# Attention and two MLPs on one core: TensorE's next instruction goes to the half of the rows that a count calls free first

## The chip, the cores and the metric

The kernel runs on one core of one Trainium2 chip. The metric is the device time of one execution in microseconds (us); the kernel before takes 653.88 us, the median of three runs (653.44 to 654.54).

## The reference, cut to what matters

```python
def _attn_ref(q, k, v):                      # (2, 8, 1152, 64) each
    q_pool = q.reshape(B, H, S // 2, 2, D).mean(axis=3)
    scores = np.matmul(q_pool, k.transpose(0, 1, 3, 2)) / np.sqrt(D)
    scores = scores - np.max(scores, axis=-1, keepdims=True)
    attn = np.exp(scores)
    attn = attn / (np.sum(attn, axis=-1, keepdims=True) + 1e-09)
    return np.matmul(attn, v)

x = attn_out.transpose(0, 2, 1, 3).reshape(1152, 512)
x = (s * np.maximum(x @ w_in, 0) ** 2 + b) @ w_out          # d_ff 2048
x = ((x @ w_a) * (x @ w_b)) @ w_out2                        # d_ff 1536
```

The change touches the attention alone: 16 heads of 576 pooled queries by 1152 keys, 64 deep, in float32.

## The kernel before, in words

The heads are worked off in eight pairs. A pair has nine blocks of 128 queries (four of each head, and one that holds the last 64 queries of both). For one block *g* the steps, with the names of the table SCHED, are:

- **S** (`s_mm`): scores against 1024 of the keys, two float32 matmuls of 512 columns. The contraction is 64 deep, so one matmul uses the lower half of TensorE's rows (partitions 0 to 63, the even chunks of keys) and the other the upper half (64 to 127, the odd chunks); the two run at the same time. **SX** (`s_mmx`): the last 128 keys, one matmul in one half only; both halves hold these keys, and before, odd blocks use the upper half and even blocks the lower.
- **M, MX, C** (VectorE): maximum over the scores; **X, XX** (ScalarE): exp with its sum; **A, R** (VectorE): the sum's reciprocal; **N** (GpSimd): the row is scaled.
- **T** (`p_tr`): the scaled block is transposed chunk by chunk, 64 rows of it at a time: eight transposes in the lower half into one PSUM tile, eight in the upper half into another. **H** copies the lower half's tile to `pt` (ScalarE, line 357), **D** the upper half's (VectorE, line 353). There is one such tile for each half, so the next group of transposes in a half waits for that copy.
- **U.0 to U.3** (`turns`): the transposes of the ninth chunk of several blocks, with those of the next pair's keys or queries riding along; **UH** and **UD** copy them out.
- **P0, P1** (`pv_mm`): attention times values, over all 128 rows.

SCHED is one period of a software pipeline, written out by hand; the marks behind a name say how many pairs it lags. `steps()` expands it, and each step is recorded in that order, so every engine's queue is in the order of the program. An engine waits for another by semaphores; TensorE adds to its semaphore behind the last transpose of each half (for H and for D) and behind the second half of an S.

In every step before, the halves simply take turns: `turn` issues lower, upper, lower, upper, and S lower, upper. The place in the period on which most turns is, in the table, `SX.8 T.4 S.7 SX.7 ... U.1 ... P0.0`: on TensorE an SX, a group of 16 transposes, an S, another SX, the 14 transposes of U.1, and then P0. It comes once in each pair's period. Behind the attention stand the two MLPs, in full rows, which the change doesn't touch.

Of the kernel before, what the change touches and what calls it, by code (L numbers as in the profile page):

```python
# [9 lines left out]
F32 = mybir.dt.float32  # L10
# [26 lines left out]
def kernel(  # L37
# [14 lines left out]
    nc = tc.nc  # L52
    B, H, S, D = q.shape
# [24 lines left out]
    ident = const.tile([128, 128], F32, name="ident")  # L78
# [176 lines left out]
    s01 = ctx.enter_context(ExitStack())  # L255
    ps_s01 = s01.enter_context(tc.tile_pool(name="ps_s01", bufs=2, space=PSUM))
# [3 lines left out]
    NE = 7  # L260
    e_all = nc.alloc_sbuf_tensor("e", [128, 3, S], F32, side="right")
    qp_all = nc.alloc_sbuf_tensor("qpl", [128, 9, 2, D], F32, side="right")
    e_at = [e_all.ap()[:, i] for i in range(3)]
# [13 lines left out]
    def bank(key, reads):  # L277
        held[key] = [free.pop(0), reads]
        return banks[held[key][0]].tile([128, 512], F32, tag="b", name="b")
# [6 lines left out]
    QN, QM, KN, VN, X, Q, QT = {}, {}, {}, {}, {}, {}, {}  # L286
    HALF = [slice(0, 64), slice(64, 128)]

    def bh(n):
        return n // HP, 2 * (n % HP)  # L290

    def load_q(n, part=0, queue=nc.sync):
        if n >= NP:
            return
        b, h = bh(n)
        if part < 2:
            QN[n] = nat.tile([128, 2, 4, 2, D], F32, tag="qn", name="qn")
        o = slice(max(part - 1, 0), 2 if part != 1 else 1)
        queue.dma_start(
            out=QN[n][:, o], in_=q[b, h + o.start:h + o.stop, 0:1024, :].rearrange("h (p j r) d -> p h j r d", p=128, j=4)  # L300
        )
        if part != 1:
            QM[n] = nat.tile([128, 2, D], F32, tag="qm", name="qm")
            for i in range(2):
                queue.dma_start(out=QM[n][HALF[i]], in_=q[b, h + i, 1024:S, :].rearrange("(p r) d -> p r d", r=2))

    def load_k(n, part=0):
        if n >= NP:
            return
        b, h = bh(n)  # L310
        if part < 2:
            KN[n] = k_p.tile([128, 2, NC + 1, D], F32, tag="kn", name="kn")
        o = slice(max(part - 1, 0), 2 if part != 1 else 1)
        src = k[b, h + o.start:h + o.stop].rearrange("h (p c) d -> p h c d", p=128)
        nc.sync.dma_start(out=KN[n][:, o, 0:NC], in_=src)
        nc.sync.dma_start(out=KN[n][:, o, NC], in_=src[:, :, NC - 1])

    def load_v(n):
        if n >= NP:
            return  # L320
        b, h = bh(n)
        VN[n] = v_p.tile([128, 2, NC, D], F32, tag="vn", name="vn")
        nc.sync.dma_start(out=VN[n], in_=v[b, h:h + 2].rearrange("h (p c) d -> p h c d", p=128))
# [11 lines left out]
    def q_step(n, hd):  # L335
        q_pool(n, hd)
        if hd == 1:
            q_pool(n, 2)
            load_q(n + 1)

    def turn(ps, z, src):
        for o, t in zip(HALF, ps):
            nc.tensor.transpose(t[:, z * 64:z * 64 + 64], src(o), ident[o, o])  # L343

    def by_half(t, n, k):
        return t.rearrange("p (m k e) -> p k m e", m=n, k=2)[:, k]
# [15 lines left out]
    SPS, XPS, SM, PS = {}, {}, {}, {}  # L362

    def s_parts(g):
        n, i = divmod(g, 9)
        hd, j = ORDER[i]

        def mm(ps, w, r, c):
            o = HALF[r]
            if hd < 2:  # L370
                nc.tensor.matmul(ps[:, 0:w], Q[n, hd][o, j * 128:(j + 1) * 128], X[n, hd][o, c], start=True, stop=True)  # L371
            else:
                for a in range(2):
                    nc.tensor.matmul(ps[HALF[a], 0:w], Q[n, 2][o, a], X[n, a][o, c], start=True, stop=True, skip_group_check=True)  # L374

        return mm

    def s_mm(g):
        SPS[g] = ps = ps_s01.tile([128, 2, 512], F32, tag="s01", name="s01")
        for r in range(2):  # L380
            s_parts(g)(ps[:, r], 512, r, slice(0, 512))

    def s_mmx(g):
        XPS[g] = ps = bank(("x", g), 2)
        s_parts(g)(ps, 128, g % 2, slice(512, 640))

    def small(g):
        if g not in SM:
# [36 lines left out]
    def t_tiles(key):  # L425
        PS[key] = [p.tile([128, 512], F32, tag="t", name="t") for p in ps_t]
        return PS[key]

    def p_turn(ps, g, z, pos):
        turn(ps, z, lambda o: e_at[g % NE][o, pos * 128:(pos + 1) * 128])  # L430

    def p_tr(g):
        ps = t_tiles(g)
        for pos in range(8):
            p_turn(ps, g, pos, pos)

    def p_col(j):
        return j * 128 if j < 2 else j * 128 + NX
# [13 lines left out]
    def turns(n, u):  # L452
        at = TURN[u] if n >= 0 else ()
        if not at and n + 1 >= NP:
            return
        ps = t_tiles((n, u))
        for z, i in enumerate(at):
            p_turn(ps, 9 * n + i, z, 8)
        if n + 1 < NP:
            z, hd = len(at), u // 2  # L460
            if u % 2:
                src = qp_all.ap()
                for j in range(4):
                    turn(ps, z + j, lambda o: src[o, 4 * hd + j].rearrange("p a d -> p (a d)"))
                if hd:
                    turn(ps, z + 4, lambda o: src[o, 8].rearrange("p a d -> p (a d)"))
                    Q[n + 1, 2] = q_p.tile([128, 2, 64], F32, tag="qt", name="qt")
                Q[n + 1, hd] = q_p.tile([128, 512], F32, tag=f"q{hd}", name="q")
            else:

                for m in range(5):
                    turn(ps, z + m, lambda o: KN[n + 1][o, hd, 2 * m:2 * m + 2].rearrange("p a d -> p (a d)"))
                X[n + 1, hd] = x_p.tile([128, 640], F32, tag=f"x{hd}", name="x")
                if hd:
                    load_k(n + 3)

    def turns_last(n, u, k):
        if n < 0:
# [18 lines left out]
    def turns_out(k):  # L497
        def run(n, u):
            turns_last(n, u, k)
            turns_ride(n, u, k)  # L500

        return run
# [4 lines left out]
    def pv_mm(n, hd, pos):  # L507
        if pos == 0:
            PV[n, hd] = bank(("pv", n, hd), 4 if (n, hd) == (NP - 1, 1) else 1)
        ps = PV[n, hd]  # L510
        for a in range(2):
            nc.tensor.matmul(  # L512
                ps[HALF[a], 0:HC], VN[n][:, hd, CHUNK[pos]], pt[:, hd, pos, a * HC:(a + 1) * HC],
                start=(pos == 0), stop=(pos == NC - 1), skip_group_check=True,
            )
        if hd and pos == NC - 1:
            load_v(n + 2)
# [34 lines left out]
    def block(f, *z):  # L552
        return lambda n, i: f(9 * n + i, *z)

    def conv_until(n, i):
# [3 lines left out]

    STEPS = dict(  # L560
        S=block(s_mm), SX=block(s_mmx), M=block(s_max), MX=block(s_maxx), C=block(s_comb), X=block(s_exp), XX=block(s_expx),
        A=block(s_add), R=block(s_rec), N=block(s_norm), T=block(p_tr), H=block(p_evac, 0), D=block(p_evac, 1),
        U=turns, UH=turns_out(0), UD=turns_out(1), QP=q_step, PVc=pv_copy, PVd=pv_move, XS=x_split, CV=conv_until,
    )
    for name in ("MM", "Fa", "Fd", "Fp"):
        STEPS[name] = lambda n, i: next(up_down)
    for hd in range(2):
        STEPS[f"P{hd}"] = lambda n, pos, hd=hd: pv_mm(n, hd, pos)

    def steps():  # L570

        lag = [(t.rstrip("',"), t.count("'") - t.count(",")) for t in SCHED]
        lags = [s for _, s in lag]
        first = dict(QP=1, CV=NP - 1, MM=NP - 1, Fa=NP - 1, Fd=NP - 1, Fp=NP - 1, U=-1, UH=-1, UD=-1)
        for p in range(min(lags) - 1, NP + max(lags)):
            for t, s in lag:
                if first.get(t.split(".")[0], 0) <= p - s < NP:
                    yield t, p - s

    def step(t, n):  # L580
        name, i = t.split(".")
        STEPS[name](n, int(i))
# [12 lines left out]
    with tc.manual_schedule():  # L595
# [13 lines left out]
        for t in early:  # L609
            step(t, -1)  # L610
# [4 lines left out]
        unit_load()  # L615
        load_v(1)
        order = [(t, n) for t, n in steps() if n >= 0 or t not in early]
        end = 1 + max(i for i, (t, n) in enumerate(order) if t.split(".")[0] in ("S", "SX"))
        for t, n in order[:end]:
            step(t, n)  # L620
# [150 lines left out]
        for t, n in order[end:]:  # L771
            step(t, n)
# [19 lines left out]
        def pair(i):  # L792
            return ps2[i].tile([128, 2, 512], F32, tag="pp", name="pp")
# [22 lines left out]
        U = {}  # L816
# [43 lines left out]
        at = [at_t[:, i] for i in range(2)]  # L860
# [26 lines left out]
        def o_room(i):  # L887
            return ab_at(i)[:, 256 + NX:256 + NX + DM]
# [17 lines left out]
        a, c, b, d = (pair(i) for i in range(4))  # L906
# [37 lines left out]
        for n in range(1, NU):  # L944
# [3 lines left out]
            a = pair(2)  # L948
# [46 lines left out]
        ps = [t[:, i] for t in (pair(i) for i in (2, 3, 1, 0)) for i in range(2)]  # L995
# [21 lines left out]
        o = o_room(8)  # L1017
# [33 lines left out]
```

## Time and profile before

| what | number |
|---|---|
| median of the runs | 653.88 us |
| the profiled execution | 653.54 us, of which the span of its instructions is 651.8 us |
| TensorE matmul busy | 637.7 us, 98% of the span |
| VectorE, ScalarE, GpSimd busy | 464.9, 332.5 and 276.5 us |
| TensorE's granted clock | full in all 40 slices |
| attention | from the start to some 238 us |
| one pair's period in the steady part | 27.74 to 27.80 us |

The page cuts the span into 40 slices and gives each engine's busy share. The timeline lists instructions in order of time: start, length, engine, line, operation, how many were merged into the row, and in brackets how long the engine had been idle and what ended it. Matmuls overlap, since a record runs from the start to the last result; where two halves work, rows of both lie over each other. A float32 matmul of 512 or 128 columns makes two passes and has two records, a transpose has one. Line numbers are those of the kernel before.

### The profile page before, as it was taken

The page shows a single profiled execution, that of the slowest core. Times are in us where ns is not written, and L with a number is a line of the kernel's source. Part 1 is how long each engine was busy: PE and PEld are TensorE (multiplying, and loading weights), DVE is VectorE, ACT ScalarE, POOL GpSimd, SP SyncE. Part 2 cuts the span into 40 slices and gives each one's busy share as a digit, 9 for nine tenths or more (in the row PEclk, how much of TensorE's full clock was granted, in tenths as well). Part 3 has the DMA queues.
Part 4 walks back from the last instruction along what each step waited for, and adds up shares of the span by engine and source line. Part 5 has one row for each costly group of instructions (what it writes and reads, how often), then busy time and mean ns, then how long its engine had stood idle before and what let it go on. Part 6 is the DMA issues. An engine that isn't in the chain of part 4 may idle for free.

```text
span 651.8 us, 13010 instructions
## 1 busy us (share of the span) xinstructions
PE 637.7 (98%) x5182; PEld 537.6 (82%) x5182; DVE 464.9 (71%) x892; ACT 332.5 (51%) x697; POOL 276.5 (42%) x228
## 2 busy tenths in 40 slices
PE   7899999999999999999999999999999999999997
PEld 5556666565665679999999999999999999988885
DVE  5888888888888845735456465889887887796431
ACT  4777778778787724535224224244434343533321
POOL 3545466564654566855355354200542453230000
PEclk9999999999999999999999999999999999999999
DMA  8313140431302044232232132500323131323004
GB/s 264 105 41 98 37 133 19 115 91 45 93 8 60 10 140 129 75 121 65 67 127 65 66 129 66 180 15 0 131 69 126 65 130 66 130 71 123 1 0 146
DMA packets 30509, 55.75 MB, mean 86 GB/s; under 512 B 4336, under 2 KB 7280, under 8 KB 30448
## 3 DMA queue, kind: packets, MB, share of 16 engines
q1 hardware_dynamic: 29920, 54.19, 25.8%
q8 instruction: 41, 0.67, 0.4%
q10 hardware_dynamic: 528, 0.72, 0.3%
q14 instruction: 20, 0.16, 0.1%
HBM read 50.33 MB, written 2.36 MB: 81 GB/s over the span
## 4 chain that ended last, share of the span: by engine, by line
PE 92%; DVE 4%; ACT 2%; POOL 1%; issue 1%; POOLq 0%; DVEq 0%; ACTq 0%
PE ps L592 31%; PE pp L592 18%; PE pp L885 11%; PE b L512 11%; PE t L343 9%; PE s L371 8%; PE b L371 2%; PE s L374 1%; DVE sm L393 1%; ACT e L406 1%; PE t L606 1%; DVE e L827 1%; PE b L374 0%; POOL e L423 0%; DVE wl L160 0%
## 5 line engine op out<-in xcount | busy, mean ns | idle before, releaser
L423 POOL TENSOR_SCALAR e<-e,sm 128x1152 f32<-128x1152 f32 x72 | 87.8, 1225 | 89.2 <-DVE sm L401 57.4
L393 DVE TENSOR_REDUCE sm<-s 128x1 f32<-128x1024 f32 x72 | 87.9, 1220 | 10.8 <-PE s L371 6.6
L406 ACT ACTIVATE e<-s,sm 128x1024 f32<-128x1024 f32 x72 | 80.5, 1118 | 13.6 <-DVE sm L401 12.7
L343 PEld LDWEIGHTS t<-ident,e 64*128 64x128 f32 x1296 | 59.1, 138 | 29.3 <-issue 9.7
L512 PE MATMUL b<-pt,vn 128*64 128x288 f32 x576 | 81.8, 416 | 0.1
L371 PE MATMUL s<-x,q 64*128 64x512 f32 x256 | 72.8, 624 | 3.1 <-ACT e L406 2.5
L353 DVE COPY pt<-t 128x512 f32<-128x512 f32 (+1 forms) x112 | 59.7, 539 | 22.0 <-PE t L343 21.8
L900 POOL TENSOR_TENSOR ab<-ab,at 128x576 f32<-128x576 f32 x24 | 35.0, 1480 | 91.1 <-ACT ab L895 87.2
L343 PE MATMUL t<-ident,e 64*128 64x64 f32 x1296 | 69.4, 228 | 4.3 <-POOL e L423 2.4
L512 PEld LDWEIGHTS b<-pt,vn 128*64 128x64 f32 x576 | 36.6, 136 | 31.9 <-ACT e L410 6.1
L357 ACT COPY pt<-t 128x512 f32<-128x512 f32 (+1 forms) x112 | 51.5, 469 | 19.3 <-PE t L343 18.6
L699 POOL TENSOR_SCALAR r<-r,sb_s,sb_b 128x384 f32<-128x384 f32 (+1 forms) x46 | 38.9, 856 | 51.8 <-DVE r L696 51.8
L693 ACT ACTIVATE qpl<-ps 128x384 f32<-128x384 f32 (+1 forms) x46 | 21.7, 503 | 69.4 <-PE ps L592 64.6
L696 DVE SCALAR_TENSOR_TENSOR r<-ps,qpl 128x384 f32<-128x384 f32 (+1 forms) x46 | 25.1, 571 | 38.4 <-ACT qpl L693 38.4
L136 ACT ACTIVATE f<-raw 128x1024 f32<-128x1024 f32 x34 | 38.6, 1135 | 17.7 <-issue 11.1
L592 PE MATMUL ps<-xa_h,wh 128*128 128x384 f32 (+1 forms) x200 | 45.3, 330 | 0.0
L592 PE MATMUL ps<-xa_h,wl 128*128 128x384 f32 (+1 forms) x200 | 45.0, 329 | 0.0
L592 PE MATMUL ps<-xa_l,wh 128*128 128x384 f32 (+1 forms) x200 | 45.0, 328 | 0.0
L140 DVE SCALAR_TENSOR_TENSOR f<-raw,f 128x1024 int32<-128x1024 int32 x34 | 43.0, 1263 | 1.1
L592 PE MATMUL ps<-gh,wh 128*128 128x384 f32 x192 | 43.7, 336 | 0.0
L592 PE MATMUL ps<-gh,wl 128*128 128x384 f32 x192 | 43.7, 336 | 0.0
L592 PE MATMUL ps<-gl,wh 128*128 128x384 f32 x192 | 43.7, 336 | 0.0
(115 smaller groups left out, 1490.3 us busy)
## 6 DMA issues: line engine op xcount, KB each, us to landing
raw<-in_moe_w_out_dram SPq DMA_DIRECT2D x14, 1024.0 KB, 4.9
raw<-in_moe_w_in_dram SPq DMA_DIRECT2D x8, 1024.0 KB, 5.4
raw<-in_moe_w_a_dram SPq DMA_DIRECT2D x6, 1024.0 KB, 5.1
raw<-in_moe_w_b_dram SPq DMA_DIRECT2D x6, 1024.0 KB, 5.1
vn<-in_v_dram SPq DMA_DIRECT2D x8, 576.0 KB, 5.9
kn<-in_k_dram SPq DMA_DIRECT2D x7, 576.0 KB, 3.9
qn<-in_q_dram SPq DMA_DIRECT2D x7, 512.0 KB, 3.8
xs<-tmp SPq DMA_DIRECT2D x30, 72.0 KB, 4.9
```

Of the source, the lines that this page charges most:

```text
L140: nc.vector.scalar_tensor_tensor(out=f, in0=lo, scalar=29, in1=f, op0=ALU.logical_shift_right, op1=ALU.bitwise_or)
L343: nc.tensor.transpose(t[:, z * 64:z * 64 + 64], src(o), ident[o, o])
L353: nc.vector.tensor_copy(out=out, in_=in_)
L357: nc.scalar.copy(out=out, in_=in_)
L371: nc.tensor.matmul(ps[:, 0:w], Q[n, hd][o, j * 128:(j + 1) * 128], X[n, hd][o, c], start=True, stop=True)
L393: nc.vector.reduce_max(small(g)[:, 0:1], SPS[g], axis=AX.XY)
L406: nc.scalar.activation(out=out, in_=SPS.pop(g), func=AF.Exp, bias=m[:, 2:3], accum_out=m[:, 4:5])
L423: nc.gpsimd.tensor_scalar(out=e, in0=e, scalar1=m[:, 6:7], scalar2=1.0, op0=ALU.mult, op1=ALU.mult)
L512: nc.tensor.matmul(ps[HALF[a], 0:HC], VN[n][:, hd, CHUNK[pos]], pt[:, hd, pos, a * HC:(a + 1) * HC], start=(pos == 0), stop=(pos == NC - 1 ...
L592: nc.tensor.matmul(ps, a, c[:, o:o + n], start=(first and z == 0), stop=(last and z == 2), skip_group_check=more)
L699: nc.gpsimd.tensor_scalar(out=r2, in0=r2, scalar1=sb_s, scalar2=sb_b, op0=ALU.mult, op1=ALU.add)
L885: nc.tensor.matmul(ps, a[x], w2_at[kf][c], start=(kf == 0 and y == 0), stop=(kf == KF2 - 1 and y == 2))
```

## The change

While the program is written, three numbers are kept: for each half, when it would be free, and when the last instruction was issued. A transpose counts 63, a half of S 960, an SX 218. `lanes` takes a list of instructions for each half and always issues next the one whose half is free first. The SX goes to the half that is free first, instead of by the block's number. `together` levels the count, before P and around the ninth block. The order of the steps is kept, with one exception: where a group T is followed by its S with nothing between that this S needs, `look_ahead` puts the two into one list, so that one half may start its S while the other still has transposes to issue.

```diff
+    clock = [0, 0, 0]
+
+    def lanes(*todo):
+        todo = [list(x) for x in todo]
+        while todo[0] or todo[1]:
+            r = min((r for r in range(2) if todo[r]), key=lambda r: (clock[r], len(todo[r]) < len(todo[1 - r])))
+            cost, run = todo[r].pop(0)
+            clock[2] = max(clock[r], clock[2])
+            clock[r] = clock[2] + cost
+            run()
+
+    def together():
+        clock[:] = [max(clock)] * 3
+
     def turn(ps, z, src):
-        for o, t in zip(HALF, ps):
-            nc.tensor.transpose(t[:, z * 64:z * 64 + 64], src(o), ident[o, o])
+        def one(o, t):
+            return 63, lambda: nc.tensor.transpose(t[:, z * 64:z * 64 + 64], src(o), ident[o, o])
+
+        return [one(o, t) for o, t in zip(HALF, ps)]
...
+    def s_halves(g):
+        SPS[g] = ps = ps_s01.tile([128, 2, 512], F32, tag="s01", name="s01")
+        mm = s_parts(g)
+        return [[(960, lambda r=r: mm(ps[:, r], 512, r, slice(0, 512)))] for r in range(2)]
+
     def s_mm(g):
-        SPS[g] = ps = ps_s01.tile([128, 2, 512], F32, tag="s01", name="s01")
-        for r in range(2):
-            s_parts(g)(ps[:, r], 512, r, slice(0, 512))
+        if g in SPS:
+            return
+        if g % 9 == 4:
+            together()
+        lanes(*s_halves(g))
 
     def s_mmx(g):
         XPS[g] = ps = bank(("x", g), 2)
-        s_parts(g)(ps, 128, g % 2, slice(512, 640))
+        if g % 9 == 4:
+            together()
+        r = int(clock[1] < clock[0])
+        todo = [[], []]
+        todo[r] = [(218, lambda: s_parts(g)(ps, 128, r, slice(512, 640)))]
+        lanes(*todo)
+        if g % 9 == 4:
+            together()
...
     def p_tr(g):
         ps = t_tiles(g)
-        for pos in range(8):
-            p_turn(ps, g, pos, pos)
+        todo = turns_both([p_turn(ps, g, pos, pos) for pos in range(8)])
+        if g in AHEAD:
+            for x, y in zip(todo, s_halves(AHEAD[g])):
+                x += y
+        lanes(*todo)
...
@@ def pv_mm(n, hd, pos):
+        together()
...
+    def look_ahead(order):
+
+        for i, (t, n) in enumerate(order):
+            name, z = t.split(".")
+            if name != "T":
+                continue
+            wait = set()
+            for u, m in order[i + 1:]:
+                next_name, y = u.split(".")
+                g = 9 * m + int(y)
+                if next_name in ("SX", "T", "U", "P0", "P1", "MM"):
+                    break
+                if next_name == "S":
+                    if y != "4" and not wait & {("X", g - 2), ("U", g // 9 - 1)}:
+                        AHEAD[9 * n + int(z)] = g
+                    break
+                wait.add(("X", g) if next_name == "X" else ("U", m) if next_name in ("UH", "UD") else None)
```

`turns` (U) gathers its transposes in the same way and hands them to `lanes`. The queues of the other engines and of the DMAs keep their order; only names of buffers differ there.

On TensorE, the first steady place `SX.8 T.4 S.7 SX.7 U.1` stood so before (b is an SX, the transposes t read the scaled block e_96, s_927 is the S; lower and upper half take turns in each row of more than one; in brackets the semaphores that the first instruction of a row waits for):

```order
L371 MATMUL b<-x,q 128x128 [waits Activation_49]
L343 MATMUL t<-ident,e_96 128x64 [waits PE_49,Pool_49]
L343 MATMUL t<-ident,e_96 128x64 [waits DVE_49]
L343 MATMUL t<-ident,e_96 128x64 x14
L371 MATMUL s_927<-x,q 128x512 [waits Activation_49]
L371 MATMUL s_927<-x,q 128x512
L371 MATMUL b<-x,q 128x128 [waits Activation_49]
```

And it stands so in the changed kernel, where the same S is called s_911; the first SX is in the lower half here:

```order
L392 MATMUL b<-x,q 128x128 [waits Activation_49]
L359 MATMUL t<-ident,e_96 128x64 [waits DVE_49,Pool_49]
L359 MATMUL t<-ident,e_96 128x64 x3
L359 MATMUL t<-ident,e_96 128x64 [waits PE_49]
L359 MATMUL t<-ident,e_96 128x64 x8
L392 MATMUL s_911<-x,q 128x512 [waits Activation_49]
L359 MATMUL t<-ident,e_96 128x64 x3
L392 MATMUL s_911<-x,q 128x512
L392 MATMUL b<-x,q 128x128 [waits Activation_49]
```

The first four transposes are now all in the upper half, the S of the upper half has moved ahead of three transposes, and these three are the last of the lower half.

A place with an S and one SX ahead of U (here U.0's transposes: e and e_93 are blocks of this pair, kn the next pair's keys) stood so before:

```order
L371 MATMUL s_785<-x,q 128x512 x2
L371 MATMUL b<-x,q 128x128
L343 MATMUL t<-ident,e 128x64 x2
L343 MATMUL t<-ident,e_93 128x64 x2
L343 MATMUL t<-ident,kn 128x64 x10
L512 MATMUL b<-pt,vn 64x288 x4
```

In the changed kernel, where this S is s_766, it stands so:

```order
L392 MATMUL s_766<-x,q 128x512 x2
L392 MATMUL b<-x,q 128x128
L359 MATMUL t<-ident,e 128x64
L359 MATMUL t<-ident,e_93 128x64
L359 MATMUL t<-ident,kn 128x64 x2
L359 MATMUL t<-ident,e 128x64
L359 MATMUL t<-ident,kn 128x64
L359 MATMUL t<-ident,e_93 128x64
L359 MATMUL t<-ident,kn 128x64 x7
L512 MATMUL b<-pt,vn 64x288 x4
```

The half without the SX has been moved ahead by four transposes; its last four no longer stand at the end, where those of the other half are now alone.

## Rows read from the trace of the kernel before

**Rows 1.** The page: busy time of the engines, and granted clock in 40 slices.

```profile
PE 637.7 (98%) x5182; PEld 537.6 (82%) x5182; DVE 464.9 (71%) x892; ACT 332.5 (51%) x697; POOL 276.5 (42%) x228
PEclk9999999999999999999999999999999999999999
```

**Rows 2.** Busy time in two periods: PE, PEld, DVE, ACT, POOL, PEclk, DMA share, GB/s.

```profile
57.29:85.09 27.80, 27.78 (x334) 17.15 (x336) 23.89 (x65) 21.36 (x58) 15.96 (x15) 1.00 0.28 80
85.09:112.83 27.74, 27.72 (x335) 17.16 (x336) 23.80 (x65) 21.45 (x58) 15.82 (x15) 1.00 0.28 78
```

**Rows 3.** The timeline of TensorE from SX.8 to P0.0, first SX in the upper half.

```profile
110.42 0.37 PE L371 MATMUL b<-x,q 64*128 64x128 f32 x1
110.52 0.28 PE L343 MATMUL t<-ident,e 64*128 64x64 f32 x1
...
111.08 0.65 PE L371 MATMUL s<-x,q 64*128 64x512 f32 x1
111.12 0.29 PE L343 MATMUL t<-ident,e 64*128 64x64 f32 x2
111.24 1.07 PE L371 MATMUL s<-x,q 64*128 64x512 f32 x3
...
112.19 0.40 PE L343 MATMUL t<-ident,e 64*128 64x64 f32 x6
...
112.76 0.46 PE L512 MATMUL b<-pt,vn 128*64 128x288 f32 x2
```

**Rows 4.** The same place a period earlier, first SX in the lower half.

```profile
82.62 0.37 PE L371 MATMUL b<-x,q 64*128 64x128 f32 x1
82.73 0.27 PE L343 MATMUL t<-ident,e 64*128 64x64 f32 x1
...
83.32 0.69 PE L371 MATMUL s<-x,q 64*128 64x512 f32 x1
83.38 0.22 PE L343 MATMUL t<-ident,e 64*128 64x64 f32 x1
...
84.35 0.22 PE L343 MATMUL t<-ident,e 64*128 64x64 f32 x1
...
85.02 0.46 PE L512 MATMUL b<-pt,vn 128*64 128x288 f32 x2
```

**Rows 5.** ScalarE's timeline at both places: the copy H.4, then XX.8 and X.8.

```profile
111.39 0.59 ACT L357 COPY pt<-t 128x512 f32<-128x512 f32 x1 [0.22 <-PE t L343]
...
83.64 0.58 ACT L357 COPY pt<-t 128x512 f32<-128x512 f32 x1 [0.27 <-PE t L343]
84.12 0.37 ACT L410 ACTIVATE e<-b,sm 128x128 f32<-128x128 f32 x1
```

**Rows 6.** VectorE's timeline at both places: C.8, then the copy D.4.

```profile
111.28 0.15 DVE L401 TENSOR_REDUCE sm<-sm 128x1 f32<-128x2 f32 x1
111.44 0.69 DVE L353 COPY pt<-t 128x512 f32<-128x512 f32 x1
...
83.47 0.15 DVE L401 TENSOR_REDUCE sm<-sm 128x1 f32<-128x2 f32 x1
83.67 0.69 DVE L353 COPY pt<-t 128x512 f32<-128x512 f32 x1
```

**Rows 7.** GpSimd's timeline: N.4, the scaling of the block that T.4 reads.

```profile
109.24 1.22 POOL L423 TENSOR_SCALAR e<-e,sm 128x1152 f32<-128x1152 f32 x1 [3.82 <-DVE sm L401]
```

**Rows 8.** TensorE's timeline in the first pair: T.4, and P0.0 after it.

```profile
27.12 0.71 PE L343 MATMUL t<-ident,e 64*128 64x64 f32 x16 [1.64 <-POOL e L423]
...
29.32 0.47 PE L512 MATMUL b<-pt,vn 128*64 128x288 f32 x2
```

**Rows 9.** TensorE's timeline, T, S, SX and U.0 up to P1: SX in the upper half.

```profile
74.03 0.71 PE L343 MATMUL t<-ident,e 64*128 64x64 f32 x16
...
76.24 0.46 PE L512 MATMUL b<-pt,vn 128*64 128x288 f32 x2
```

**Rows 10.** The same place a period later, SX in the lower half.

```profile
101.83 0.71 PE L343 MATMUL t<-ident,e 64*128 64x64 f32 x16
...
104.03 0.46 PE L512 MATMUL b<-pt,vn 128*64 128x288 f32 x2
```

More of the change, by code (lines that the diff above doesn't have):

```diff
@@ L339, in q_step, with turns_both @@
             load_q(n + 1)
-    def turn(ps, z, src):
-        for o, t in zip(HALF, ps):
-            nc.tensor.transpose(t[:, z * 64:z * 64 + 64], src(o), ident[o, o])
+    clock = [0, 0, 0]
[9 more added lines that the diff above has]
+        clock[:] = [max(clock)] * 3
+    def turn(ps, z, src):
+        def one(o, t):
+            return 63, lambda: nc.tensor.transpose(t[:, z * 64:z * 64 + 64], src(o), ident[o, o])
+        return [one(o, t) for o, t in zip(HALF, ps)]
+    def turns_both(items):
+        return [[x[r] for x in items] for r in range(2)]
     def by_half(t, n, k):
@@ L429, in p_turn @@
     def p_turn(ps, g, z, pos):
-        turn(ps, z, lambda o: e_at[g % NE][o, pos * 128:(pos + 1) * 128])
+        return turn(ps, z, lambda o: e_at[g % NE][o, pos * 128:(pos + 1) * 128])
+    AHEAD = {}
     def p_tr(g):
         ps = t_tiles(g)
-        for pos in range(8):
-            p_turn(ps, g, pos, pos)
+        todo = turns_both([p_turn(ps, g, pos, pos) for pos in range(8)])
[3 more added lines that the diff above has]
+        lanes(*todo)
     def p_col(j):
@@ L456, in turns @@
         ps = t_tiles((n, u))
-        for z, i in enumerate(at):
-            p_turn(ps, 9 * n + i, z, 8)
+        items = [p_turn(ps, 9 * n + i, z, 8) for z, i in enumerate(at)]
         if n + 1 < NP:
@@ L462, in turns @@
                 src = qp_all.ap()
-                for j in range(4):
-                    turn(ps, z + j, lambda o: src[o, 4 * hd + j].rearrange("p a d -> p (a d)"))
+                for j in [4 * hd + j for j in range(4)] + [8] * hd:
+                    items.append(turn(ps, len(items), lambda o, j=j: src[o, j].rearrange("p a d -> p (a d)")))
                 if hd:
-                    turn(ps, z + 4, lambda o: src[o, 8].rearrange("p a d -> p (a d)"))
                     Q[n + 1, 2] = q_p.tile([128, 2, 64], F32, tag="qt", name="qt")
@@ L471, in turns @@
                 for m in range(5):
-                    turn(ps, z + m, lambda o: KN[n + 1][o, hd, 2 * m:2 * m + 2].rearrange("p a d -> p (a d)"))
+                    items.append(turn(ps, z + m, lambda o, m=m: KN[n + 1][o, hd, 2 * m:2 * m + 2].rearrange("p a d -> p (a d)")))
                 X[n + 1, hd] = x_p.tile([128, 640], F32, tag=f"x{hd}", name="x")
-                if hd:
-                    load_k(n + 3)
+        lanes(*turns_both(items))
+        if u == 2:
+            load_k(n + 3)
     def turns_last(n, u, k):
@@ L617 @@
         order = [(t, n) for t, n in steps() if n >= 0 or t not in early]
+        look_ahead(order)
         end = 1 + max(i for i, (t, n) in enumerate(order) if t.split(".")[0] in ("S", "SX"))
```

## The prediction, made before the changed kernel ran

> **What bounds the kernel now.** I read the page's busy shares first. TensorE is busy for 98% of the span, and its granted clock is full in every slice, the level of 2.4 GHz [rows 1]. Then I cut the attention into stretches of one pair: the steady periods take 27.74 to 27.80 us, and TensorE is busy in all but 0.02 us of each, while VectorE has 23.8 to 23.9, ScalarE 21.4 and GpSimd 15.8 to 16.0 [rows 2]. So a steady period ends when TensorE is through its queue, and what TensorE waits for or gains there goes into the total. It says little of one half, though: with two halves at work, TensorE counts as busy when either is. So I went to the timeline and followed each half through the places where the change moves most.
>
> The reader is to see three things there. First, the halves are not held in program order when they start. At 83.32 the upper half's S begins, and one transpose, at 83.38, begins after it [rows 4]; it can only be the lower half's last, since a half keeps its own order, and in the program before it stands ahead of both halves of that S. So TensorE already lets the half that is free go ahead.
>
> Second, results are reported in program order, over both halves. In rows 3 the lower half's S starts at 111.08, so that half's last transpose started earlier and, at 0.22 long, was over by 111.30 at the latest. ScalarE sat idle for 0.22 and waited for it, yet its copy H.4 begins at 111.39 [rows 5]. What ended 0.05 before is the first of the two late transposes (111.12 + 0.22 = 111.34), an upper one that stands ahead of the lower half's last. In rows 4 it is the other way: the upper half was through its transposes by 83.32 + 0.22 = 83.54, VectorE was through with C.8 at 83.47 + 0.15 = 83.62, but D.4 begins at 83.67 and H.4 at 83.64 [rows 5, 6], both just behind the end of the lower half's last one, 83.38 + 0.22 = 83.60. Where nothing of that sort is in the way, D.4 follows C.8 by 0.01 (111.43 to 111.44).
>
> Here a rule of the Trainium skill is weighed. "TensorE: Matmul & The Clock Gate" says in Part 3, under The mechanism, that matmuls start and end strictly in program order, with no reordering. The trace disagrees on the starts (83.32 before 83.38) and agrees on the ends as far as these four copies show. If starts were in order too, the time below would be the same, for the three transposes that count would wait for the start of an S, not for its end.
>
> Third, at this place the copies matter: U.1's transposes need the PSUM tiles that H.4 and D.4 empty, so 112.19 is 0.06 behind D.4's end (111.44 + 0.69 = 112.13) [rows 3, 6].
>
> **The change, part by part.** The count adds no instruction: TensorE has the same matmuls, and no other queue changes its order, DMA queues included. So everything hangs on the order within TensorE.
>
> *One SX beside transposes.* The half without SX gets up to four transposes ahead. The half with the SX is the longer one and stays so; its work is the same. Before, it makes no difference which half that is: from the first T to P1 it is 76.24 - 74.03 = 2.21 us with the SX in the upper half and 104.03 - 101.83 = 2.20 in the lower [rows 9, 10]. I take 0 for all these places. What hides the new order is the longer half; bounds, from the starts 0.06 to 0.11 apart in rows 3, 4 and 8: a start gained or lost at each of some 30 places, 2 us either way at the very most, and I see no reason for either sign.
>
> *S ahead of transposes (T.4 with S.7).* This is one place in each of the eight pairs. The upper half's S now stands ahead of the last three (in the first pair two) transposes of the lower half. By the second finding H.4 can't be released before that S has ended. I count from the start of the first SX:
>
> - T.4 waits for N.4 as before (109.24 + 1.22 = 110.46 [rows 7]); its first transpose is at 0.10 or 0.11 [rows 3, 4]. I take 0.11.
> - Eight transposes of one half: a group of 16 takes 0.71 from first start to last end [rows 8], less 0.22 for the last one's length and with 0.06 to the next start, 0.55. So the upper S starts at 0.66.
> - One half of an S, first start to end: 1.07 (the row at 111.24 ends with the upper half's second pass [rows 3]). It ends at 1.73.
> - H.4 is released 0.04 later (83.60 to 83.64), at 1.77, where before it was at 111.39 - 110.42 = 0.97 and 83.64 - 82.62 = 1.02.
> - H.4 takes 0.59 [rows 5]: 2.36. U.1's first transpose follows by 0.06: 2.42. The upper half's transposes stand behind it in TensorE's queue, and so P0 behind both.
> - From U.1's first transpose to P0.0 it is 112.76 - 112.19 = 0.57 [rows 3]: 2.99.
>
> Before, P0.0 came at 2.34 (first SX in the upper half) and 85.02 - 82.62 = 2.40 (lower) [rows 3, 4]. So TensorE loses 0.65 or 0.59 there, with nothing to do: S.7 and SX.7 are done by some 1.8. Seven pairs have the place so, four of the first kind (the last pair included, with fewer transposes behind it) and three of the second: 4 x 0.65 + 3 x 0.59 = 4.37. In the first pair T.4 starts at 27.12; the same steps give 27.12 + 0.55 + 1.07 + 0.04 + 0.59 + 0.06 + 0.57 = 30.00 against 29.32 [rows 8], 0.68. Together 5.05 us.
>
> What is hung behind H.4 on ScalarE: XX.8 and X.8. XX.8 starts 0.48 after H.4 (83.64 to 84.12) and takes 0.37 [rows 5], so it would be done at 2.62, ahead of P0.0, which needs its bank: no further loss by 0.37. VectorE's D.4 is free earlier, and M.7 waits for the lower S, which keeps its time; so VectorE is not held. The gain that the move is for, the upper half's S at 0.66 and no longer at 111.24 - 110.42 = 0.82 or 83.32 - 82.62 = 0.70, is swallowed in the same wait.
>
> The sum: the profiled span 651.8 + 5.05 = 656.85, with the 1.74 around it (653.54 - 651.8) 658.59. The median of the runs is 0.34 above the profiled execution: 658.9.
>
> Bounds of the one cost that no row shows, a transpose reported behind an S of the other half: from below, H.4 released by its own half as if nothing stood ahead, which leaves the place bounded by D.4 (C.8's end at 1.01, 0.69, 0.06, then 0.57: 2.33, a gain of 0.01 and 0.07); from above, the whole delay of H.4 (0.75 to 0.80) passed on eight times, 6.4. The four copies stand near the first reading, so I take 5.05 and keep both ends.
>
> **The rivals.**
>
> *The halves are independent, in their reports too, when one runs an S.* For it: the four copies show transposes behind transposes only, none behind an S of two passes. Against it: all four obey program order. The time: 4 x 0.01 + 3 x 0.07 = 0.25 less, some 653.6; if D.4 didn't bind either, some 0.1 to 0.15 at eight places, 652.8. "TensorEngine Tiling (Array Packing)" of the Trainium skill states under Key Properties that tiles operate independently; by that alone this rival would hold.
>
> *The order does nothing, since TensorE takes the free half by itself.* For it: the start at 83.32. Against it: the copies go by the program's order. 653.9.
>
> *The late H.4 spreads.* X.8 starts later by all of H.4's delay, 0.80, and with it the copies UH.1 behind it on ScalarE, which T.5 needs. For it: ScalarE's queue is in order. Against it: ScalarE has over 6 us free in a period [rows 2]. If it takes hold, each place costs the whole 0.80: 8 x 0.80 = 6.4, 660.3.
>
> *Slack takes part of it.* Waits for ScalarE or GpSimd elsewhere in the period may become shorter by what TensorE is late. For it: GpSimd's 3.82 idle before N.4. Against it: TensorE is idle only 0.02 per period. If a third goes, 3.4 remain: 657.2.
>
> **How the numbers follow.** The smallest difference that a measurement of this kernel can tell is about 0.2%, 1.3 us. My forecast, 658.9 with its own range 658.0 to 659.8, has 0.50. Slack 0.18, spreading 0.15, together with it 0.83, all slower. Independent reports 0.10 and no effect 0.07: 0.13 of these lie within 0.2%, 0.04 are faster by more. The range from 655.5 to 660.6 leaves out the last two rivals' 0.17 and little else.
>
> **What would show it.** In the changed profile: at the eight places ScalarE's copy of the lower half's tile begins right behind the end of the upper half's S, some 0.75 later than before, while VectorE's copy comes no later; TensorE then stands for about half a microsecond ahead of U.1's transposes, with that copy as what ends the wait; the period grows to some 28.4; the other places and the MLPs keep their times. The prediction is wrong if H.4 starts near 1.0 behind the first SX, or if the wait is there and the period still takes 27.8.

## The result: slower by 0.8%, and the profile after

The changed kernel takes 659.14 us in the median of four runs (658.39 to 660.61) against 653.75 for the kernel before (653.44 to 654.54): a ratio of 1.0084, 95% interval 1.0068 to 1.0099. Its profiled execution spans 656.8 us where the prediction's sum gave 656.85.

Busy shares and clock say nothing of it: the page of the changed kernel reads nearly as [rows 1] did, with TensorE 1.4 us busier and the clock full in every slice.

```profile
PE 639.1 (97%) x5182; PEld 536.1 (82%) x5182; DVE 464.2 (71%) x892; ACT 334.4 (51%) x697; POOL 276.8 (42%) x228
PEclk9999999999999999999999999999999999999999
```

Two steady periods, cut from P0.0 to P0.0 as in [rows 2] and with the same columns, show where the time lies: each is 0.63 to 0.69 longer, and now has 0.50 us without any matmul where before it had 0.02.

```profile
58.41:86.84 28.43, 27.93 (x336) 16.94 (x332) 23.83 (x65) 21.65 (x58) 15.91 (x15) 1.00 0.28 78
86.84:115.27 28.43, 27.93 (x336) 16.95 (x332) 23.84 (x65) 21.65 (x58) 15.92 (x15) 1.00 0.29 78
```

The list of waits names it. Each row gives who waits for whom, the total in us, how often, and the longest. Of the kernel before, the waits of U's transposes for ScalarE's copy of a tile:

```profile
PE t L343 <- ACT pt L357: 1.9, 3, 0.8
```

And of the changed kernel:

```profile
PE t L359 <- ACT pt L378: 4.5, 9, 0.7
```

Before, two of the three are in the last pair's tail (0.82 and 0.67 on TensorE's timeline there); now there is one in every pair. TensorE's timeline at one of the steady places, which answers to [rows 3, 4]:

```profile
55.40 0.37 PE L392 MATMUL b<-x,q 64*128 64x128 f32 x1
55.51 0.27 PE L359 MATMUL t<-ident,e 64*128 64x64 f32 x1
...
56.06 0.65 PE L392 MATMUL s<-x,q 64*128 64x512 f32 x1
56.09 0.28 PE L359 MATMUL t<-ident,e 64*128 64x64 f32 x2
56.22 1.07 PE L392 MATMUL s<-x,q 64*128 64x512 f32 x3
56.97 0.38 PE L392 MATMUL b<-x,q 64*128 64x128 f32 x2
57.83 0.40 PE L359 MATMUL t<-ident,e 64*128 64x64 f32 x6 [0.48 <-ACT pt L378]
...
58.41 0.46 PE L552 MATMUL b<-pt,vn 128*64 128x288 f32 x2
```

ScalarE there, H.4 and then XX.8, which answers to [rows 5]:

```profile
57.19 0.59 ACT L378 COPY pt<-t 128x512 f32<-128x512 f32 x1 [1.04 <-PE t L359]
57.68 0.38 ACT L445 ACTIVATE e<-b,sm 128x128 f32<-128x128 f32 x1
```

VectorE there, C.8 and then D.4, which answers to [rows 6]:

```profile
56.25 0.15 DVE L436 TENSOR_REDUCE sm<-sm 128x1 f32<-128x2 f32 x1
56.32 0.68 DVE L374 COPY pt<-t 128x512 f32<-128x512 f32 x1
```

The reader is to see one odd thing: the last two lower transposes start at 56.09 and, by their records, are over by 56.37, and ScalarE, idle for 1.04, does not begin to copy their tile before 57.19. What ended just ahead of that is the upper half's S: it began at 56.06 and its second pass ends 1.07 later, at 57.13. VectorE's copy of the upper tile begins at 56.32, right after the upper transposes, which are ahead of that S. The trace also keeps the times at which TensorE's semaphore is raised, and they say the same: 56.23 for the upper transposes, 57.17 for the lower ones, 57.31 for the S. So it is the report that is late, not the copy. From here it is as worked out: H.4 ends at 57.78, U.1 follows at 57.83, P0.0 at 58.41.

From the start of the first SX to P0.0 that is 3.01; measured from the last P ahead of the place to P0.0, it is 3.35 at the six steady places, against 2.67 or 2.74 before: 0.67 more where the first SX was in the upper half before, 0.61 where it was in the lower. The last pair loses 0.60. In the first pair P0.0 comes at 29.98 and not at 29.32 [rows 8]:

```profile
27.08 0.77 PE L359 MATMUL t<-ident,e 64*128 64x64 f32 x16 [1.80 <-POOL e L458]
...
29.40 0.40 PE L359 MATMUL t<-ident,e 64*128 64x64 f32 x6 [0.47 <-ACT pt L378]
29.98 0.46 PE L552 MATMUL b<-pt,vn 128*64 128x288 f32 x2
```

Together 3 x 0.67 + 3 x 0.61 + 0.60 + 0.66 = 5.10. One stretch in the second pair, near 36.6, is 0.17 shorter: in the kernel before, the T there waited for GpSimd's N, which ended at 37.01, and began at 37.06; TensorE now comes there 0.68 later and finds N done. All other stretches are within 0.03, and in 419 us of the MLPs TensorE is busy for 414.32 against 414.26. The places with one SX beside transposes, where most of the diff is at work, take 2.20 as before [rows 9, 10]:

```profile
103.67 0.71 PE L359 MATMUL t<-ident,e 64*128 64x64 f32 x16
...
105.87 0.46 PE L552 MATMUL b<-pt,vn 128*64 128x288 f32 x2
```

### The profile page after: what moved, and what is told of

Read it like the earlier page. It is cut to its first block, busy times and chain, and to the rows that moved or that the text cites. A ratio compares the mean times of both kernels' runs of the same rounds, so it can differ in the third digit from the quotient of the medians.

```text
span 656.8 us, 13004 instructions
## 1 busy us (share of the span) xinstructions
PE 639.1 (97%) x5182; PEld 536.1 (82%) x5182; DVE 464.2 (71%) x892; ACT 334.4 (51%) x697; POOL 276.8 (42%) x228
## 4 chain that ended last, share of the span: by engine, by line
PE 92%; DVE 4%; ACT 2%; issue 1%; POOL 0%; DVEq 0%; POOLq 0%; ACTq 0%
PE ps L650 31%; PE pp L650 18%; PE b L552 12%; PE pp L944 11%; PE t L359 10%; PE s L392 8%; PE b L392 2%; PE s L395 1%; ACT e L441 1%; ACT pt L378 1%; DVE sm L428 1%; PE t L664 1%; DVE e L886 1%; PE b L395 0%; POOL e L458 0%
## 5 line engine op out<-in xcount | busy, mean ns | idle before, releaser
L359 PEld LDWEIGHTS t<-ident,e 64*128 64x128 f32 x1296 | 56.2, 138 | 33.5 <-POOL e L458 12.4
```

Of the source, the lines that this page charges most:

```text
L359: return 63, lambda: nc.tensor.transpose(t[:, z * 64:z * 64 + 64], src(o), ident[o, o])
```

## Experiments

The theory: a half's instructions may start ahead of older ones of the other half, but a transpose reports to the engine that waits for its tile only when every matmul ahead of it in the program, of either half, has ended. So the S that `look_ahead` moves up holds back the report of the transposes behind it, and with it H.4, U.1 and P0. The rivals: the halves report independently and something else in the change costs the time (the other reordering, or the S taking away a slot), or the late copy is only partly what TensorE waits for. "Place" below is the stretch from the last P ahead of SX.8 to P0.0. It is read from one profiled execution each; the ratios are of all runs.

**The changed kernel without `look_ahead`.** The count and `lanes` stay.

```diff
-        look_ahead(order)
```

> The changed kernel without the look-ahead: the count still sets the order inside every step and the half of the SX, but no S stands ahead of a transpose any more. Theory 1 (TensorE reports in program order, so the moved S holds back the copy H.4 at eight places): the whole loss is gone, 653.5 to 653.8; H.4 starts about 1.0 behind the first SX, the wait ahead of U.1 is gone. Rival 2 (the order by the count costs by itself: four transposes of one half in a row, the SX always in the lower half): stays near 658 to 659. Rival 3 (both in equal parts): about 656.

Measured: 653.89 us, ratio to before 0.9996 (0.9985 to 1.0008), span 652.1. The whole loss is gone, so it is `look_ahead`'s alone. In TensorE's timeline there is no wait ahead of U.1:

```profile
83.53 0.65 PE L392 MATMUL s<-x,q 64*128 64x512 f32 x1
83.57 0.28 PE L359 MATMUL t<-ident,e 64*128 64x64 f32 x2
...
84.61 0.39 PE L359 MATMUL t<-ident,e 64*128 64x64 f32 x6
...
85.18 1.68 PE L552 MATMUL b<-pt,vn 128*64 128x288 f32 x12
86.79 0.80 PE L359 MATMUL t<-ident,e 64*128 64x64 f32 x16
```

And ScalarE's H.4 is back to 1.01 behind the first SX (82.88):

```profile
83.89 0.59 ACT L378 COPY pt<-t 128x512 f32<-128x512 f32 x1 [0.27 <-PE t L359]
```

TensorE's starts at the place are the same as in the changed kernel, counted from the first SX: the upper half's S at 0.65 (0.66 there), the last two lower transposes at 0.69 (0.69). What differs is which of them stands first in the program, and with it H.4 goes from 1.79 to 1.01. So the transposes don't start late in the changed kernel; they are reported late.

The places are 2.64 to 2.65 long, 0.02 to 0.10 shorter than before, which is the small gain that the reordering by itself could bring. It is lost again at once: the next group, T.5, takes 0.80 and not 0.72, and the stretch with it is 0.04 to 0.08 longer. So the even count of the halves is worth nothing here. One half's transposes in T.5 begin 0.12 behind the other's, when VectorE's semaphore is raised; why VectorE comes no earlier is not shown.

**The kernel before with nothing but that move.** In T.4, five pairs of transposes, the other three upper ones, the upper half of S.7, the last three lower ones, the lower half of S.7. Here and below `s_mm` is skipped where the S was already issued; the cuts show each half by its number and leave out the lines that choose T.4 and make the tile `s`.

```diff
-        for pos in range(8):
-            p_turn(ps, g, pos, pos)
+        for pos in range(5):
+            one(0, pos)
+            one(1, pos)
+        for pos in range(5, 8):
+            one(1, pos)
+        s_parts(g + 3)(s[:, 1], 512, 1, slice(0, 512))
+        for pos in range(5, 8):
+            one(0, pos)
+        s_parts(g + 3)(s[:, 0], 512, 0, slice(0, 512))
```

> The kernel before with one edit: in T.4 the last three transposes of the lower half stand behind the upper half's S.7; all else takes turns as before, and the SX goes by the block's number. Theory 1: the upper S starts 0.82 (first SX in the upper half) or 0.66 (lower) behind the first SX, ends 1.07 later, H.4 follows by 0.04 and takes 0.59, U.1 0.06, P0.0 0.57: 3.15 or 2.99 in place of 2.34 or 2.40. 4 x 0.81 + 3 x 0.59 + 0.68 = 5.7 more: 659.4. Rival 2: no loss, 653.8.

Measured: 659.16 us, ratio 1.0075 (1.0057 to 1.0093), span 657.0. The places are 0.835 longer with the first SX in the upper half and 0.645 with it in the lower. So the move alone, in the old kernel, brings the loss. It costs more than the change does at a place of the first kind (0.67 there), since the upper S starts 0.81 behind the first SX and not 0.66. The last pair loses 0.86. In the first pair, T.4 to P0.0 is 0.71 longer, but T.4 began 0.55 earlier in this execution (26.57 for 27.12), which the move doesn't explain; without that the span would be some 657.5, and not so near to the changed kernel's. TensorE at a place of the first kind:

```profile
112.69 0.65 PE L371 MATMUL s<-x,q 64*128 64x512 f32 x1
112.75 0.22 PE L440 MATMUL t<-ident,e 64*128 64x64 f32 x1
112.81 1.07 PE L371 MATMUL s<-x,q 64*128 64x512 f32 x3
...
114.47 0.40 PE L343 MATMUL t<-ident,e 64*128 64x64 f32 x6 [0.36 <-ACT pt L357]
115.05 0.46 PE L529 MATMUL b<-pt,vn 128*64 128x288 f32 x2
```

ScalarE's H.4 in it:

```profile
113.83 0.59 ACT L357 COPY pt<-t 128x512 f32<-128x512 f32 x1 [1.20 <-PE t L440]
```

The S starts at 112.69 and its second pass ends 1.07 later, at 113.76, 0.07 ahead of the copy. The last lower transpose began at 112.75 and was over by 112.97.

**Only one transpose behind the S.** As above, with seven pairs.

```diff
-        for pos in range(5):
+        for pos in range(7):
             one(0, pos)
             one(1, pos)
-        for pos in range(5, 8):
+        for pos in range(7, 8):
             one(1, pos)
```

> As the run with three transposes behind the S, but only the very last transpose of the lower half stands behind it. Theory 1: one is enough, since the copy waits for the last one alone and that is reported behind the S: again 5.7 more, 659.4. Rival 4 (the price is that of the transposes themselves, which are held up behind the S): a third of the loss, about 655.7, or nothing.

Measured: 661.20 us, ratio 1.0101 (1.0084 to 1.0118), span 658.7. The steady places are 0.82 and 0.63 longer, almost the same as with three: it is not the number of transposes moved that costs, but that the last one of the tile is behind the S. ScalarE's H.4 and, under it, TensorE at the same place:

```profile
115.57 0.59 ACT L357 COPY pt<-t 128x512 f32<-128x512 f32 x1 [1.19 <-PE s L371]
```

```profile
114.44 1.08 PE L371 MATMUL s<-x,q 64*128 64x512 f32 x4
```

The 1.7 us that the span has beyond the last kernel's are elsewhere, in the first pair. T.4 begins there at 27.12, as before, and not 0.55 earlier. From T.4 to P0.0 it is 4.17 and not 2.91 (the passes of S take 2.02 in all, before 1.08), while the granted clock fell to the lower of the two levels, 1.2 GHz: busy time by microsecond, columns as in [rows 2].

```profile
27.00:28.00 1.00, 0.88 (x18) 0.88 (x18) 1.00 (x4) 0.50 (x2) 1.00 (x2) 0.61 0.00 0
28.00:29.00 1.00, 1.00 (x8) 0.48 (x7) 0.79 (x3) 0.00 (x0) 1.00 (x3) 0.50 0.00 0
```

TensorE had stood idle for 1.64 us ahead of it, waiting for N.4, exactly as before [rows 8], where the clock stayed full. So this part isn't the place's. Nor is it shown to be the order's: the mean granted clock of this execution, 0.997, is also that of 4 of the 17 executions of the kernel before. And two of the four executions of this kernel have 0.999 and 1.000 and still span 659.4, so what lifts its median 2 us above the last kernel's stays open.

**The mirror.** The lower half of S.7 ahead of the last three upper transposes. If the program's order decides, D.4 is held now and H.4 is free.

```diff
-        for pos in range(5, 8):
-            one(1, pos)
-        s_parts(g + 3)(s[:, 1], 512, 1, slice(0, 512))
-        for pos in range(5, 8):
-            one(0, pos)
-        s_parts(g + 3)(s[:, 0], 512, 0, slice(0, 512))
+        for pos in range(5, 8):
+            one(0, pos)
+        s_parts(g + 3)(s[:, 0], 512, 0, slice(0, 512))
+        for pos in range(5, 8):
+            one(1, pos)
+        s_parts(g + 3)(s[:, 1], 512, 1, slice(0, 512))
```

> The mirror image: the lower half's S.7 stands ahead of the last three transposes of the upper half, so VectorE's copy D.4 should be held back and ScalarE's H.4 not. Theory 1: D.4 starts 1.77 or 1.93 behind the first SX (before: 1.01 to 1.05), takes 0.69, then 0.06 and 0.57 to P0.0: 3.09 or 3.25. 4 x 0.75 + 3 x 0.85 + 0.78 = 6.3 more, 660.0; VectorE is the busier engine and M.7 stands behind D.4, so up to 662. Rival 5 (something of ScalarE or of the lower half alone): no loss here, 653.8.

Measured: 659.64 us, ratio 1.0084 (1.0065 to 1.0102), span 657.6; the places are 0.77 and 0.88 longer. The wait has changed sides. ScalarE's H.4, 0.85 behind the first SX (112.31):

```profile
113.16 0.59 ACT L357 COPY pt<-t 128x512 f32<-128x512 f32 x1
```

VectorE's D.4, 1.78 behind it:

```profile
114.09 0.69 DVE L353 COPY pt<-t 128x512 f32<-128x512 f32 x1 [0.79 <-PE t L440]
```

And TensorE, whose wait is now ended by VectorE:

```profile
112.96 0.65 PE L371 MATMUL s<-x,q 64*128 64x512 f32 x1
...
114.84 0.40 PE L343 MATMUL t<-ident,e 64*128 64x64 f32 x5 [0.53 <-DVE pt L353]
```

The copy that is late is the one whose transposes stand behind the other half's S, whichever half that is. Nothing about ScalarE or the lower half does it.

**A shorter instruction in the way.** As the second experiment, but the upper half's S is cut: 256 columns ahead of the three lower transposes, the other 256 last. The same work on TensorE, and half as much to end ahead of the report.

```diff
-        s_parts(g + 3)(s[:, 1], 512, 1, slice(0, 512))
+        s_parts(g + 3)(s[:, 1, 0:256], 256, 1, slice(0, 256))
         for pos in range(5, 8):
             one(0, pos)
         s_parts(g + 3)(s[:, 0], 512, 0, slice(0, 512))
+        s_parts(g + 3)(s[:, 1, 256:512], 256, 1, slice(256, 512))
```

> As the run with three transposes behind the upper half's S, but that S is cut in two: 256 columns stand ahead of the three transposes, 256 behind them. Theory 1: the copy H.4 waits for the first piece alone, 0.64 from its first start to its end (1.07 less 0.43 for 256 columns fewer in each of two passes), and not 1.07: each place loses 0.43 less than with the whole S (0.84 and 0.65 there): 4 x 0.41 + 3 x 0.22 + 0.25 = 2.5 more than before, about 656.5. Rival 4 (what counts is that an S stands there at all): as with the whole S, 659.

Measured: the places are 0.41 and 0.22 longer, down from 0.835 and 0.645. The profiled span is 653.9, 2.1 above before's; the ratio is 1.0016 (1.0003 to 1.0029), about 1 us, with the runs of the kernel before scattered over 3.5 us. I rest the verdict on the places. TensorE:

```profile
111.79 0.43 PE L371 MATMUL s<-x,q 64*128 64x256 f32 x1
...
113.14 0.40 PE L343 MATMUL t<-ident,e 64*128 64x64 f32 x6
```

H.4 on ScalarE, 1.53 behind the first SX (110.97), between 0.97 before and 1.95 with the whole S ahead:

```profile
112.50 0.58 ACT L357 COPY pt<-t 128x512 f32<-128x512 f32 x1 [0.79 <-PE t L440]
```

The delay goes with the length of the matmul in the way. That is the size of the loss shown, not only its place.

**Starts: how far a half looks past the other.** In every T of the kernel before, all eight lower transposes stand ahead of all eight upper ones. If starts were free, the halves would still run beside each other.

```diff
-        for pos in range(8):
-            p_turn(ps, g, pos, pos)
+        for r in range(2):
+            for pos in range(8):
+                nc.tensor.transpose(... HALF[r] ...)
```

> The kernel before with one edit: in every T all eight transposes of the lower half stand ahead of all eight of the upper half. Theory 1 says of starts only that TensorE lets the free half go ahead. If it looks over the whole group, 653.8 as before. If it can pass only two waiting instructions of the other half (as the starts in the trace of before suggest), the upper half starts when five or six lower ones have gone, 0.3 to 0.37 later, in 64 groups of 16, and part of it is hidden by the S that follows: 10 to 24 us more, 664 to 678.

Measured: 667.75 us, ratio 1.0192 (1.0165 to 1.0218), span 666.2; the stretches with a T are 0.12 to 0.42 longer (0.05 at the last pair's place). A whole group takes 0.96 where it took 0.71 [rows 8]; under it, the busy time of another T and the number of its transposes at work in the first and the second quarter of a microsecond (columns: stretch, length, busy and count, clock, DMA share, GB/s):

```profile
85.18 0.96 PE L436 MATMUL t<-ident,e 64*128 64x64 f32 x16
```

```profile
88.47:88.72 0.25, 0.23 (x4) 1.00 0.00 0
88.72:88.97 0.25, 0.25 (x10) 1.00 0.00 0
```

Four transposes are at work in the first quarter and ten in the second, three of these left over from the first: one half runs first, then both. The upper half's first starts about 0.25 behind the lower half's first, when the lower half's fifth has begun. Three lower ones, the sixth to the eighth, stand between them. The lower half's S behind this T, too, starts only when no more than three upper transposes are left:

```profile
89.04 0.69 PE L371 MATMUL s<-x,q 64*128 64x512 f32 x1
89.10 0.35 PE L436 MATMUL t<-ident,e 64*128 64x64 f32 x3
```

One half thus gets ahead of about three that still wait, where the expectation had two, and 64 groups where there are 72. Starts are free within a short reach and not beyond. Of the 14.4 us that the span has beyond before's, 2.7 lie ahead of the first pair's P0, where here too the granted clock fell to 0.50 for some 3 us; the other 11.7 come at full clock.

**The changed kernel with a shorter copy.** In seven pairs H.4 copies four of the eight chunks only; the other four of those 64 queries are left out. It asks whether H.4 is what TensorE waits for, with its full length.

```diff
+        if g % 9 == 4 and g > 9 and not k:
+            copy(k, out[:, 0:4], slots(PS[g], k, 0, 4))
+            return
         copy(k, out, slots(PS[g], k, 0, 8))
```

> The changed kernel, but H.4 copies four of eight chunks in seven of the eight pairs (the other four chunks of those 64 queries are left out). Theory 1: the wait ahead of U.1 ends with H.4, so what H.4 gets shorter comes off the time: a copy of 512 columns takes 0.59, of 128 some 0.27, so of 256 about 0.38, 0.21 less, at seven places 1.5: about 657.5. Rival 6 (U.1 waits for something else, the S itself or X.8): no change, 659.

Measured: the places are 3.125 to 3.135 long, 0.22 shorter than the changed kernel's, and the copy itself is 0.22 shorter (0.37 for 0.59). The span is 655.3, 1.5 less than the changed kernel's 656.8: 7 x 0.22. The ratio to before is 1.0056 (1.0038 to 1.0074). H.4 on ScalarE:

```profile
85.49 0.37 ACT L378 COPY pt<-t 128x256 f32<-128x256 f32 x1 [1.05 <-PE t L359]
```

TensorE, from the upper half's S to U.1:

```profile
84.35 0.65 PE L392 MATMUL s<-x,q 64*128 64x512 f32 x1
...
85.91 0.40 PE L359 MATMUL t<-ident,e 64*128 64x64 f32 x6 [0.27 <-ACT pt L378]
```

The copy starts as late as before it was cut, 1.79 behind the first SX (83.70), and all of the 0.22 taken from it comes off the place. The chain from S's end over H.4 and U.1 to P0 is the bound, with no slack within these 0.22.

## Why the prediction was right

*That starts pass each other and reports don't.* The step on which all else rested was read from four copies, none of them behind an S. It holds: H.4 or D.4 begins 0.05 to 0.07 behind the end of the S ahead of its last transpose, for three transposes or one, for either half, and sooner when the S is cut.

One of the four copies was misread: D.4 at 111.44 [rows 6] didn't wait for C.8, since in the changed kernel D.4 begins at 56.32, ahead of the end of C.8's record at 56.40. It follows its own transposes, for which TensorE's semaphore was raised at 111.42. That leaves the rule as it is and lowers only the bound from below, which took D.4 to begin no earlier than C.8's end.

"TensorE: Matmul & The Clock Gate" of the Trainium skill has matmuls start and end in program order (Part 3, The mechanism). The ends agree: every copy here goes by them. The starts don't, within a short reach, and there the measurement decides: 83.38 behind 83.32 [rows 4], and the kernel with the halves in blocks. "TensorEngine Tiling (Array Packing)" of the Trainium skill has tiles operate independently (Key Properties). That holds for the starts and not for what the other engines are told. None of the runs shows whether the transposes' results lie in PSUM earlier than they are reported.

*The steps of the place.* All came within 0.02: the first transpose 0.11 behind the first SX (0.11), the upper S at 0.66 (0.66), H.4 at 1.79 (1.77), U.1 at 2.43 (2.42), P0.0 at 3.01 (2.99). Only SX.7, which I had done by some 1.8, ends at 1.95; the wait is 0.48 for that.

*The sum.* 0.67 and 0.61 for 0.65 and 0.59, the first pair 0.66 for 0.68, the last 0.60 where I had counted 0.65. The sum of the eight, 5.10 for 5.05, is right because these errors are small and cancel, not because each is exact. That the span came within 0.05 is luck besides: it holds the 0.17 won in the second pair, which I hadn't counted.

*The rest at nothing.* The places with one SX keep their 2.20, and without `look_ahead` the kernel is at 0.9996. The small gains that the freer half does bring, up to 0.10 at a place, are given back at T.5; I had not named that wait. My bound of 2 us for some 30 starts goes with 0.06 for each; with the 0.11 that I also named it would be 3.3.

*The rivals.* Independent reports fall with H.4's start and with the mirror. That the order does nothing falls with the ratio. The late H.4 does not spread: XX.8 begins 0.49 behind it as before, VectorE is not held, and the other stretches stand. Slack takes 0.17 of it, once, in the second pair, by a wait for GpSimd as that rival has it, and nothing in the steady part: with the copy cut, the place follows in full. In the mirror, where VectorE is the one that is late, it spreads no further either.

## What to carry to other kernels

Where two halves of the array work side by side, sort the program by who waits for a result, not only by which half is free: put a short matmul that another engine waits for ahead of a long one of the other half, since it is reported only after what stands ahead of it has ended. Read such a wait from the start of the waiting copy, not from the end of its own matmuls. A balance of busy time over the halves is worth little where the stretch ends on another engine's copy.

## What was not expected of the hardware

A half passes only a few older instructions of the other: with eight in a row ahead, the other half starts 0.25 late. In all the groups behind the first pair's P0 that costs 11.7 us, at full clock. So taking turns in the program, which looks needless when starts are free, is worth 1.8% here.

In two of the profiled executions (one transpose behind the S, and the halves in blocks) the granted clock falls to 0.50 for some 3 us in the first pair, after TensorE stood idle for 1.64 and 1.80; in the kernel before and the changed kernel it stays full after the same two idle times. In the first of the two it cost 1.3 us, as much as two of the places. The idle time alone doesn't decide it, and no run here shows what does.
